# Turned features of the last stage: two more tiles turned on VectorE, and the blocks moved inside SBUF in place of a trip through DRAM

## The chip, the cores and the metric

The kernel runs on one NeuronCore of a Trainium2 chip. The core has TensorE (PE in the profile, its weight loads PEld), VectorE (DVE), ScalarE (ACT), GpSimd (POOL) and SyncE (SP), a scratch memory SBUF of 128 partitions, and PSUM, into which TensorE writes. Transfers are issued by an engine's queue (here mostly SP and POOL) and carried out by 16 DMA engines that all queues share. The metric is the device time of one execution in microseconds (us).

## What is computed

Two branches read the same layer-normed input, and both are added to it (sequence 2048, width 512, all in 32-bit floats):

```
xn  = layernorm(x)
q, k, v = heads(xn @ wqkv)                     # 32 heads of 16
phi(t)  = [softmax(t @ w_phi), softmax(-t @ w_phi)]   # 32 features a head
o   = phi(q) (phi(k)^T v) / (phi(q) (phi(k)^T 1) + 1e-6)
A   = o @ wo
z1, z2 = halves of gelu(xn @ w_in)             # 688 columns each
B   = (z1 * (w_sp @ layernorm(z2) + b_sp)) @ w_out
out = x + A + B
```

## The kernel before

The 2048 rows are 16 tiles of 128. Every large product is made of three matmuls: both operands are split into a rounded part (`round_h`, line 46, on ScalarE) and the rest (`rest_l`, line 51, on VectorE), and `mm3` (line 54) adds high x high, high x rest and rest x high. So in the profile L56, L57 and L58 are nearly all matmuls, L48 nearly all roundings and L52 nearly all rests.

The work has three stages. The first (about 0 to 190 us) norms and transposes x, makes q, k and v, the features of both (the exponentials and the reciprocals of their sums; the query side goes to DRAM, `e_d`, unscaled) and the sums over the keys. The second makes the w_sp product as a seven-product block scheme (`products`, `drain`, line 771 on), in 32 steps of which four make one pair of output tiles, and gates it (`gate`, line 797); the gated pair goes to DRAM already turned, features on partitions (`u_d`, `ur_d`).

The last stage, which the change is about, is the loop at line 1064, from about 485 us to the end. It takes the tiles in pairs i, i + 1. For each pair TensorE does, in this order: `project_u(i)` (gated values times w_out), `attend` (L997: 32 small matmuls of the features with the key sums), `project_u(i + 1)`, and `project_o` for both tiles (attention times wo, into the same PSUM tile). ScalarE copies the sum out (L1029), and POOL issues a store that adds it to the output, which holds x already (L1030). The next pair's attention needs its features *turned*: features on partitions, tokens along the row. How that is done depends on the tile:

- Tiles 0 and 1 are turned during the second stage: VectorE transposes every 32 x 32 block (`turn_q`, L561), four POOL stores (L563) put the blocks in their places in a DRAM buffer `q_d`, and SP loads them (L906).
- Tiles 2 to 7 (`s < TQ`, TQ = 8) stay as they are. Tiles 4 to 7 are copied by POOL into a tile of another type (L945, `er<-et`). `attend_T` (line 965) transposes them on TensorE, sixteen 128 x 128 transposes a pair (L980 for pair 2, L982 for pairs 4 and 6), and ScalarE copies the result out of PSUM in four pieces (L984).
- Tiles 8 to 15 take the way of tiles 0 and 1, but in this stage: the transpose L561, four stores of 128 KB (L563), and one load of 512 KB into the operand tile `f` (L939). The load waits for the four stores.

Before that, each tile's features are finished on VectorE (`q_fin`, line 541): a product with the key sums (L545), a reduction (L546), four small operations (L547 to L550), and the scaling of the 1024 features (L552). `ahead` (line 1054) runs behind each `project_o(i)`: it loads the features of tile i + 5 (L538), the gated values of tile i + 4 (L836, L837), and calls `features(i + 3)`. So the features of tile 11 are finished and turned while pair 8 and 9 is being projected.

The order in each engine's queue is not written out by hand: a planner runs a simulated time line over the instructions in the order of the program and puts on each queue what is ready, the earlier in the program first; `tc.issue_after(ins)` holds what follows behind one instruction of the same queue. Each queue then runs in that fixed order, and an instruction at its head that waits holds up everything behind it. The operand tiles `er` and `f` share three buffers (`er_pair`, line 925); the tile that VectorE transposes into (`qtmp`) is one of a ring of 16 (`slot`, line 825).

During this stage there is one more piece of VectorE work: the last pair's gate (line 1087, behind pair 6), whose z1 tile is loaded (line 1084) behind the transfer kept in `lasts[6]`.

Of the kernel before, what the change touches and what calls it, by code (L numbers as in the profile page):

```python
# [10 lines left out]
F32 = mybir.dt.float32  # L11
# [7 lines left out]
P = 128  # L19
S, D, H, DH, FH = 2048, 512, 32, 16, 688  # L20
NT = S // P
# [3 lines left out]
NF = 2 * D  # L25
# [3 lines left out]
BL = 32  # L29
# [11 lines left out]
def mixer(ctx: ExitStack, tc: tile.TileContext, x, x_t, wv, wqkT, phi_bd, wo, w_in, wst, b_r, w_out, out):  # L41
    nc = tc.nc
    pe, act, dve, pool, sp = nc.tensor, nc.scalar, nc.vector, nc.gpsimd, nc.sync
# [31 lines left out]
    dram = ctx.enter_context(tc.tile_pool(name="dram", bufs=1, space=DRAM))  # L75
# [3 lines left out]
    ur_d = dram.tile([NT, 2 * REM, P], F32, name="ur_d")  # L79
    kvT_d = dram.tile([P, D], F32, name="kvT_d")  # L80
    zb_d = dram.tile([P, NF], F32, name="zb_d")
    q_d = dram.tile([NT, P, NF], F32, name="q_d")
    nm_d = dram.tile([NT, ND, P], F32, name="nm_d")

    ident = cst.tile([P, P], F32, name="ident")
# [91 lines left out]
    with ExitStack() as p0:  # L177
# [236 lines left out]
        t = xz_tile(2 * D, F32R, "xT").rearrange("p (a b) -> p a b", a=2)  # L414
        xT.append(t)
        x0, pts = xt.pop(0), []
        for k in range(2):
            pts.append(ps.tile([P, 2, P], F32, tag="mm", name="pt"))
            for c in range(2):
                i = pe.transpose(pts[k][:, c], x0[:, (2 * k + c) * P:(2 * k + c + 1) * P], ident).ins  # L420
            keep(pe=i)
        warm_up(2)
        for cs, pt in zip(halves, pts):
            src = pt.rearrange("p a b -> p (a b)")
            i = round_h(act, t[:, 0, cs], src)
# [7 lines left out]
        p = ps.tile([P, D], F32, tag="mm", name="proj")  # L433
# [7 lines left out]
        p = ps.tile([P, D], F32, tag="mm", name="proj")  # L441
# [18 lines left out]
        p = ps.tile([P, D], F32, tag="mm", name="proj")  # L460
# [90 lines left out]
                          den.unsqueeze(2).to_broadcast([P, H, 2]), op=ALU.mult)  # L551
        return e, dve.tensor_tensor(heads(e), heads(e), bc(w, 2 * H), op=ALU.mult).ins  # L552

    TQ = 8

    NB = NF // P
    QB = NB * BL

    def turn_q(s, dst, e, eng):

        dve.transpose(dst.rearrange("p (m c t) -> p m c t", c=NB, t=BL), e.rearrange("p (c m j) -> p m c j", c=NB, j=BL))  # L561
        for b in range(P // BL):
            eng.dma_start(q_d[s, :, b * QB:(b + 1) * QB].rearrange("(m j) w -> j m w", j=BL),  # L563
                          dst[b * BL:(b + 1) * BL].rearrange("p (m w) -> p m w", w=QB))

    QC = 4
    NQ = NT // QC
# [45 lines left out]
    with ExitStack() as p1:  # L613
# [44 lines left out]
        for s in range(NE):  # L658
            et = load_q(s, tb.tile([P, QW], F32, name="et") if s else tmp1.tile([P, 4, D], F32, tag="zhl", name="et").rearrange("p a b -> p (a b)")[:, :QW])
            tmp = zw.tile([P, 4, FC], F32, tag="z2", bufs=2, name="qtmp").rearrange("p a b -> p (a b)")[:, :NF]  # L660
            e, _ = q_fin(et, tmp, zb)
# [57 lines left out]
    for s in range(NT):  # L719
        p = zproj((kv_ps_p, zc, zbp, za)[s % 4], s, w2, (0, 1) if s % 2 == 0 else (1, 0))  # L720
# [6 lines left out]
        z = z2[n][:, 2 * (s % 2):2 * (s % 2) + 2]  # L727
# [140 lines left out]
    for n in range(NC):  # L868
        i = SEQ[n][0]
        if n % NQ == 1 and i < NP - 1:  # L870
            z = load_z1(i)
        products(n, g)
        if n % NQ == NQ - 1 and i < NP - 1:
            c = gt.tile([P, 2, FU], F32, tag="c", name="c")
            cq = c[:, :, :FH].rearrange("p k (j f) -> p k j f", j=2)
            cb = drain(i, g, cq)
            g = {}
        if n + 3 < NC:
            raw[n + 3] = load_a(n + 3)
        if n + 2 < NC:  # L880
            A[n + 2] = prep_a(n + 2, raw.pop(n + 2))
        if n % NQ == NQ - 1 and i < NP - 1:
            turn = gate(i, cb, z, c, z, prep_a.last)
            if i < NP - 2:
                turn()
            if i in (2, 4):
                s = i // 2 - 1
                e, t = (gt.tile([P, 2, FU], F32, tag=tag, name=name).rearrange("p k f -> p (k f)")[:, :NF]
                        for tag, name in (("c", "c"), ("z1", "z1t")))
                pool.dma_start(e, e_d[s, :, :NF])  # L890
                turn_q(s, t, e, pool)
        if n == NC - 4:
            stage_w()
        if n == NC - 3:
            zs = slot("zb", F32R)
            zb, ident_r = zs[:, :NF].bitcast(F32), zs[:, NF:NF + P]
            round_h(act, ident_r, ident)
            sp.dma_start(zb, zb_d)
            uT = [first_gate(0)]
            ets[2] = load_q(2, slot("et"))  # L900
            es[2], last = q_fin(ets.pop(2), slot("qtmp")[:, :NF], zb)
        if n == NC - 2:
            fq = [slot("f")[:, :NF].rearrange("p (k b c t) -> p k b c t", k=2, c=NB // 2, t=BL) for h in range(2)]
            for k in range(2):
                for h in range(2):
                    sp.dma_start(fq[h][:, k], q_d[k].rearrange("p (b h w) -> h p b w", h=2, w=QB // 2)[h])  # L906
            t = xz_tile((KF + 1) * P, F32R, "u1")
            us = {1: load_u(1, t[:, :KF * P].bitcast(F32), t[:2 * REM, KF * P:(KF + 1) * P])}
    cb = drain(NP - 1, g, slot("c").rearrange("p (k j f) -> p k j f", k=2, j=2))
    with tc.issue_after(cb[2]):  # L910
        turn()
    mid.close()


# [13 lines left out]
    def features(s):  # L928
        with tc.issue_after(fin[-1]):
            tmp = slot("qtmp")[:, :NF]  # L930
            es[s], ins = q_fin(ets.pop(s), tmp, zb)
        fin.append(ins)
        if s == 3:
            return
        if s >= TQ:
            if s % 2 == 0:
                ft[s] = er_pair("f").bitcast(F32)
            turn_q(s, tmp, es.pop(s), pool)
            sp.dma_start(ft[s - s % 2][:, s % 2], q_d[s])  # L939
            return  # L940
        e = es[s]
        if s % 2 == 0:
            ep[s] = er_pair("er")
        es[s] = ep[s - s % 2][:, s % 2]
        lasts[6] = pool.dma_start(es[s].bitcast(F32), e).ins  # L945
# [117 lines left out]
    p, nxt = {}, dict(enumerate(uT))  # L1063
# [61 lines left out]
```

## Time and profile before

| | us |
|---|---|
| three runs, median (lowest to highest) | 620.32 (619.74 to 622.54) |
| the profiled execution | 618.58 |
| its span, first to last instruction | 616.8 |
| PE busy in the span | 607.8 |
| DVE busy in the span | 519.0 |
| ACT busy in the span | 261.5 |
| POOL busy in the span | 134.2 |

The mean granted clock of TensorE in that execution was 0.998. In rows of instructions the first numbers are the start and the length in us from the start of the span; "L561" is line 561 of the kernel, `qtmp<-et` is output and input by the program's names, and what stands in brackets is how long the engine was idle before and what ended it. A row of a group gives the count, the shortest, median and longest time in ns, and the first and last start. The rows of DMA issues give the count, the size of each, and the median us from issue to landing.

### The profile page before, as it was taken

The numbers are of one execution on the slowest core, as the hardware profiler recorded it, in microseconds if no ns is written. First come the engines' busy times: TensorE is split into PE (matmuls) and PEld (weight loads), VectorE is DVE, ScalarE is ACT, GpSimd is POOL, SyncE is SP. The second block draws the span as 40 slices with busy tenths as digits, with TensorE's granted clock in tenths as the row PEclk, the third lists the DMA queues.
The fourth block names the chain that finished last, engine by engine and source line by source line (L and its number), as shares of the span: only waits on it lengthen the run. The fifth ranks groups of instructions, "written<-read, shape, count | busy, mean of one in ns | idle before, by whom it ended". The sixth has DMA issues, their size and how long they took to land.

```text
span 616.8 us, 11392 instructions
## 1 busy us (share of the span) xinstructions
PE 607.8 (99%) x4286; PEld 554.4 (90%) x4286; DVE 519.0 (84%) x929; ACT 261.5 (42%) x416; POOL 134.2 (22%) x236
## 2 busy tenths in 40 slices
PE   8999999999999999999999999999999999999996
PEld 7888888888889999999999999999999987777775
DVE  5999999999978398989889896877879999999821
ACT  5653334323523467876434443342435343332221
POOL 4122232232110015442000002000100032344420
PEclk9999999999999999999999999999999999999999
DMA  8557876666446768001463745555566799999772
GB/s 315 192 136 165 227 178 170 159 163 169 125 143 162 255 224 289 2 1 35 149 142 124 191 96 177 135 157 145 165 182 215 214 345 306 322 272 264 188 172 58
DMA packets 58415, 109.95 MB, mean 178 GB/s; under 512 B 12457, under 2 KB 24617, under 8 KB 58121
## 3 DMA queue, kind: packets, MB, share of 16 engines
q1 hardware_dynamic: 43400, 64.96, 34.4%
q0 software_dynamic: 12656, 38.64, 25.1%
q10 hardware_dynamic: 2304, 5.64, 2.3%
q8 instruction: 33, 0.54, 0.3%
q14 instruction: 22, 0.17, 0.1%
HBM read 66.85 MB, written 35.80 MB: 166 GB/s over the span
## 4 chain that ended last, share of the span: by engine, by line
PE 95%; DMA 2%; issue 0%; DVE 0%; ACT 0%; SPq 0%; POOL 0%; DVEq 0%; ACTq 0%; POOLq 0%
PE g L58 11%; PE g L57 11%; PE g L56 11%; PE proj L57 7%; PE proj L56 7%; PE proj L58 7%; PE zps L56 6%; PE zps L57 6%; PE zps L58 6%; PE pout L56 6%; PE pout L58 5%; PE pout L57 5%; PE po L997 1%; DMA wst__2228<-in_w_in 1%; PE kvps L355 1%; PE pout L1011 1%
## 5 line engine op out<-in xcount | busy, mean ns | idle before, releaser
L57 PE MATMUL g<-B,A 128*128 128x344 f32 x448 | 143.3, 320 | 0.0
L56 PE MATMUL g<-B,A 128*128 128x344 f32 x448 | 142.9, 320 | 0.0
L58 PE MATMUL g<-B,A 128*128 128x344 f32 x448 | 140.4, 321 | 0.1
L56 PEld LDWEIGHTS g<-B,A 128*128 128x128 f32 x448 | 84.3, 188 | 0.1
L57 PEld LDWEIGHTS g<-B,A 128*128 128x128 f32 x448 | 84.2, 188 | 0.0
L58 PEld LDWEIGHTS g<-B,A 128*128 128x128 f32 x448 | 83.6, 188 | 0.4 <-DVE A L52 0.4
L48 ACT ACTIVATE A<-S 128x512 fp32r<-128x512 f32 x64 | 39.5, 630 | 78.7 <-DVE S L603 53.7
L56 PE MATMUL proj<-wqk_h,xT 128*128 128x512 f32 x128 | 50.1, 391 | 0.0
L58 PE MATMUL proj<-wqk_h,xT 128*128 128x512 f32 x128 | 49.8, 389 | 0.0
L57 PE MATMUL proj<-wqk_l,xT 128*128 128x512 f32 x128 | 49.8, 389 | 0.0
L123 ACT ACTIVATE e<-e,r_x 128x1024 f32<-128x1024 f32 x26 | 29.8, 1148 | 42.3 <-DVE e L122 41.2
L52 DVE TENSOR_TENSOR A<-S,A 128x512 fp32r<-128x512 f32 x64 | 43.0, 684 | 3.1 <-ACT A L48 2.8
L48 ACT ACTIVATE A<-wf 128x512 fp32r<-128x512 f32 (+1 forms) x64 | 32.9, 516 | 24.9 <-DMA wf<-in_wst 19.0
L56 PE MATMUL zps<-w_0h,xT 128*128 128x344 f32 x128 | 40.9, 320 | 0.1
L57 PE MATMUL zps<-w_1l,xT 128*128 128x344 f32 x128 | 40.8, 319 | 0.0
L57 PE MATMUL zps<-w_0l,xT 128*128 128x344 f32 x128 | 40.8, 319 | 0.0
L58 PE MATMUL zps<-w_0h,xT 128*128 128x344 f32 x128 | 40.8, 318 | 0.0
L56 PE MATMUL zps<-w_1h,xT 128*128 128x344 f32 x128 | 40.7, 318 | 0.0
L58 PE MATMUL zps<-w_1h,xT 128*128 128x344 f32 x128 | 40.6, 319 | 0.0
L52 DVE TENSOR_TENSOR A<-wf,A 128x512 fp32r<-128x512 f32 (+1 forms) x64 | 35.1, 551 | 3.7 <-ACT A L48 3.7
L126 DVE TENSOR_REDUCE sm<-e 128x64 f32<-128x1024 f32 x26 | 31.1, 1199 | 2.5 <-ACT e L123 2.5
L768 POOL DMA_DIRECT2D z1t<-z_d x16 | 8.7, 552 | 108.8 <-DMA wf<-in_wst 71.8
(224 smaller groups left out, 1435.4 us busy)
## 6 DMA issues: line engine op xcount, KB each, us to landing
wf<-in_wst SPq DMA_DIRECT2D x64, 256.0 KB, 3.2
e_d<-e POOLq DMA_DIRECT2D x16, 544.0 KB, 4.8
et<-e_d SPq DMA_DIRECT2D x16, 544.0 KB, 7.2
z_d<-z1f ACTq DMA_DIRECT2D x16, 344.0 KB, 3.1
z1t<-z_d POOLq DMA_DIRECT2D x16, 344.0 KB, 4.3
zacc<-e POOLq DMA_DIRECT2D x10, 512.0 KB, 4.9
u<-u_d SPq DMA_DIRECT2D x15, 320.0 KB, 4.9
xt<-in_x SPq DMA_DIRECT2D x16, 256.0 KB, 4.3
```

Of the source, the lines that this page charges most:

```text
L48: return act.activation(h, src, AF.Copy).ins
L52: return (eng or dve).tensor_tensor(l, src, h.bitcast(F32), op=ALU.subtract).ins
L56: pe.matmul(dst, ah, bh, start=start, stop=False)
L57: pe.matmul(dst, ah, bl, start=False, stop=False)
L58: return pe.matmul(dst, al, bh, start=False, stop=stop).ins
L123: softmax_pair.last = less, act.activation(e, e, AF.Exp, scale=scale).ins
L126: dve.tensor_reduce(sm, heads(e), axis=AX.X, op=ALU.add)
L355: i = pe.matmul(kv_acc[k:k + QP, m // 4], vs[:, m * QP:(m + 1) * QP], e[:, m * HP:(m + 1) * HP], start=first and m < 4 and len(ready) == n ...
L768: pool.dma_start(t[:, k, :FH], z1_d[2 * i + k])
L997: lasts[3] = pe.matmul(po[r][c * QP:(c + 1) * QP, k], kvT[rows, m // 2, cols], fs[m // 4][rows, m // 2 % 2], start=True, stop=True).ins
L1011: lasts[2] = pe.matmul(p, rt, w, start=False, stop=i == NT - 1 and k == 1).ins
```

## The change

Three things change, all in how features get turned.

1. TQ goes from 8 to 6: tiles 6 and 7 are now turned by VectorE too. Their copies L945, their sixteen TensorE transposes L982 and four ScalarE copies L984 are gone.
2. In the last stage (tiles 6 to 15) the transposed tile no longer goes to `q_d` and back. `move_q` sends each of the 4 x 4 pieces of 32 partitions x 256 elements (32 KB) straight from the transposed tile into the operand tile: sixteen transfers a tile, eight issued by SP (even b) and eight by POOL (odd b).
3. `q_d` keeps only tiles 0 and 1, whose way through DRAM stays as it was (`turn` and `store_q` together do what `turn_q` did). The name `turn` of the gate's second half becomes `turn_u`.

Since `lasts[6]` is set only where the copy L945 is issued, the load of z1 for the last gate now stands behind tile 5's copy and not tile 6's.

```diff
-    q_d = dram.tile([NT, P, NF], F32, name="q_d")
+    q_d = dram.tile([2, P, NF], F32, name="q_d")
...
-    TQ = 8
+    TQ = 6
...
-    def turn_q(s, dst, e, eng):
-
+    def turn(dst, e):
         dve.transpose(dst.rearrange("p (m c t) -> p m c t", c=NB, t=BL), e.rearrange("p (c m j) -> p m c j", c=NB, j=BL))
+
+    def store_q(s, t):
         for b in range(P // BL):
-            eng.dma_start(q_d[s, :, b * QB:(b + 1) * QB].rearrange("(m j) w -> j m w", j=BL),
-                          dst[b * BL:(b + 1) * BL].rearrange("p (m w) -> p m w", w=QB))
+            pool.dma_start(q_d[s, :, b * QB:(b + 1) * QB].rearrange("(m j) w -> j m w", j=BL),
+                           t[b * BL:(b + 1) * BL].rearrange("p (m w) -> p m w", w=QB))
+
+    def move_q(f, t):
+        for b in range(P // BL):
+            for m in range(P // BL):
+                move_q.last = (sp if b % 2 == 0 else pool).dma_start(f[m * BL:(m + 1) * BL, b * QB:(b + 1) * QB],
+                                                      t[b * BL:(b + 1) * BL, m * QB:(m + 1) * QB]).ins
...
                 pool.dma_start(e, e_d[s, :, :NF])
-                turn_q(s, t, e, pool)
+                turn(t, e)
+                store_q(s, t)
...
             if s % 2 == 0:
                 ft[s] = er_pair("f").bitcast(F32)
-            turn_q(s, tmp, es.pop(s), pool)
-            sp.dma_start(ft[s - s % 2][:, s % 2], q_d[s])
+            turn(tmp, es.pop(s))
+            move_q(ft[s - s % 2][:, s % 2], tmp)
             return
```

6 lines of the change are left out of this document (3 added, 3 removed).

## The prediction

> **What bounds the kernel now.** I read the page first (engine totals, the chain that ended last), then the last stage in stretches of 10 us, because every edited line runs there, then the chain of waits in order of time, and last the timelines of VectorE, POOL and SP around the one gap that the chain shows.
>
> ```profile
> span 616.8 us, 11392 instructions
> PE 607.8 (99%) x4286; PEld 554.4 (90%) x4286; DVE 519.0 (84%) x929; ACT 261.5 (42%) x416; POOL 134.2 (22%) x236
> ...
> PE 95%; DMA 2%; issue 0%; DVE 0%; ACT 0%; SPq 0%; POOL 0%; DVEq 0%; ACTq 0%; POOLq 0%
> ```
>
> TensorE is busy for 99% of the span and 95% of the closing chain is its own work. So a change pays only where it takes work off TensorE or closes one of its few gaps. The stretches say where a gap is; the columns are busy us of PE, PEld, DVE, ACT and POOL, then the granted clock, the busy share of the DMA engines, and GB/s.
>
> ```profile
> 540.00:550.00 10.00, 10.00 (x72) 7.60 (x71) 9.61 (x15) 3.81 (x5) 3.99 (x8) 1.00 0.97 268
> 550.00:560.00 10.00, 10.00 (x72) 7.64 (x71) 9.96 (x17) 3.03 (x5) 3.76 (x6) 1.00 1.02 270
> 560.00:570.00 10.00, 10.00 (x46) 8.17 (x44) 9.73 (x16) 2.25 (x4) 4.44 (x8) 1.00 0.94 270
> 570.00:580.00 10.00, 8.42 (x65) 6.38 (x64) 7.94 (x13) 2.25 (x4) 2.63 (x5) 1.00 0.81 222
> 580.00:590.00 10.00, 10.00 (x72) 7.67 (x71) 8.42 (x12) 3.02 (x5) 6.34 (x10) 1.00 0.77 157
> ```
>
> Here TensorE, VectorE and the DMA engines are all nearly full, and TensorE stands still once, for 1.58 us between 570 and 580. The chain of waits names the place, and the rows of L997 say for what:
>
> ```profile
> 536.09 1.34 PE ptq L982 x16
> ...
> 541.39 1.02 PE po L997 x32
> ...
> 570.34 1.58 issue
> 571.92 1.10 PE po L997 x32
> ...
> 586.47 1.02 PE po L997 x32
> ...
> 600.94 1.02 PE po L997 x32
> ```
>
> ```profile
> L997 PEldq EVENT_SEMAPHORE  x1: 5757/5757/5757, 566.1 to 566.1; - x1
> ```
>
> Every L997 group is the attention of one pair of tiles. The group at 571.92 is pair 10 and 11, and its queue stood in a semaphore wait from 566.1 to 571.86. What it waited for is the turned operand tile of tile 11, which goes VectorE transpose, four POOL stores to DRAM, SP load:
>
> ```profile
> 556.93 1.24 DVE L561 STREAM_TRANSPOSE qtmp<-et 128x1024 f32<-128x1024 f32 x1
> ```
>
> ```profile
> 558.47 2.25 POOL L563 DMA_DIRECT2D q_d<-qtmp  x4 [4.61 <-DVE qtmp L561]
> ```
>
> ```profile
> 565.53 0.34 SPq L939 DMA_DIRECT2D f<-q_d  x1
> ```
>
> The transpose ends at 558.17, the stores are issued from 558.47 to 560.72, the load can start only at 565.53, and the tile is there at 571.86: 13.7 us after the transpose, of which some 11 are two trips of a transfer.
>
> **The change part by part.** *Tiles 6 and 7 leave TensorE.* Sixteen transposes on TensorE (1.34 us at 536.09, on the path) go, and with them four ScalarE copies out of PSUM (L984), which nobody waits for because ScalarE is idle for more than half of these stretches. TensorE then reaches pair 6 at 541.39 - 1.34 = 540.05 and pair 10 at 570.34 - 1.34 = 569.0.
>
> *VectorE gets two more transposes.*
>
> ```profile
> 531.23 1.22 DVE L545 TENSOR_TENSOR qtmp<-et,zb 128x1024 f32<-128x1024 f32 x1
> ...
> 533.10 1.24 DVE L561 STREAM_TRANSPOSE qtmp<-et 128x1024 f32<-128x1024 f32 x1
> 534.26 1.18 DVE L546 TENSOR_REDUCE et<-qtmp 128x64 f32<-128x1024 f32 x1
> ...
> 573.73 1.29 DVE L52 TENSOR_TENSOR oT<-po,oT 128x512 fp32r<-128x512 f32 x2 [0.49 <-ACT oT L48]
> ...
> 577.23 0.83 DVE L52 TENSOR_TENSOR ul<-u,uh 128x640 fp32r<-128x640 f32 x1 [1.47 <-ACT uh L48]
> ...
> 585.27 1.25 DVE L561 STREAM_TRANSPOSE qtmp<-et 128x1024 f32<-128x1024 f32 x1
> ```
>
> One takes 1.16 us of the queue (533.10 to 534.26), two take 2.32. The stretches show VectorE with 9.6 to 10 us of work in every 10 up to 570, so nothing absorbs this before tile 11: its transpose ends at 558.17 + 2.32 = 560.49. Later 0.49 + 1.47 = 1.96 us of idle time (573.73, 577.23) take most of it back, so tile 15 is late by 0.36 only.
>
> *The trip through DRAM becomes one hop.* For tiles 6 to 15 sixteen transfers of 32 partitions x 1 KB replace the stores and the load; eight go through SP (even b), eight through POOL (odd b). No row shows such a transfer, so I bound its two costs. Issue: the four stores take 2.25 / 4 = 0.56 us each on POOL, and eight in a row on the same queue kept that pace, as did the 32-partition stores on SP; the rows are those, then the durations of all stores of q_d, then three of landing:
>
> ```profile
> 492.45 2.35 POOL L818 DMA_DIRECT2D u_d<-z1t  x4 [34.92 <-DVE z1t L814]
> 494.78 2.25 POOL L820 DMA_DIRECT2D ur_d<-z1t  x4
> ```
>
> ```profile
> L818 SPq DMA_DIRECT2D u_d<-zt x4: 330/518/782, 553.1 to 558.4; - x4
> ```
>
> ```profile
> L563 POOL DMA_DIRECT2D q_d<-qtmp x32: 550/572/937, 534.6 to 588.5; - x32
> ```
>
> ```profile
> wof<-in_wo SPq DMA_DIRECT2D x16, 64.0 KB, 2.9
> ```
>
> ```profile
> er<-et POOLq DMA_DIRECT2D x4, 512.0 KB, 7.7
> ```
>
> ```profile
> DMA to landing us min/median/max: 5.6/7.7/9.6
> ```
>
> So the eighth starts 7 x 0.56 = 3.9 us after the first, on POOL as on SP; the bounds are 0.33 (the shortest on SP) and 0.94 (the longest store on POOL). Landing: small loads of 64 KB took 2.9, and the one SBUF to SBUF copy of this stage, 512 KB, 7.7, with 5.6 and 9.6 as its ends (the last row is of that copy, L945). I take 5.3: that is what tile 11's own stores needed from the start of the fourth (558.47 + 3 x 0.56 = 560.15) to the load's start, less the short dispatch, under the same load on the DMA engines. It is the nearest row in shape, place and time; 2.9 and 9.6 stay as ends. Then tile 11 is there at 560.49 + 0.30 (transpose to first issue, as 558.17 to 558.47) + 3.9 + 5.3 = 570.0. TensorE arrives at 569.0 and waits 1.0 in place of 1.58; it starts pair 10 at 570.0 and not at 571.92: **1.9 us gained** in all.
>
> ```profile
> 523.75 1.23 DVE L552 TENSOR_TENSOR et<-et 128x1024 f32<-128x1024 f32 x1
> ...
> 530.09 1.22 DVE L552 TENSOR_TENSOR et<-et 128x1024 f32<-128x1024 f32 x1
> ```
>
> ```profile
> 570.16 1.24 DVE L561 STREAM_TRANSPOSE qtmp<-et 128x1024 f32<-128x1024 f32 x1
> ```
>
> ```profile
> 586.81 2.22 POOL L563 DMA_DIRECT2D q_d<-qtmp  x4 [0.74 <-DVE qtmp L561]
> ```
>
> ```profile
> 595.01 0.32 SPq L939 DMA_DIRECT2D f<-q_d  x1
> ```
>
> The other pairs by the same terms. Tile 13 (transpose 570.16 + 1.24 = 571.40): 571.40 + 2.32 + 0.30 + 3.9 + 5.3 = 583.2, needed at 586.47 - 1.9 = 584.6. Tile 15: 585.27 + 1.25 + 0.36 + 0.30 + 3.9 + 6.5 (what its own stores took, from 588.47 to the load at 595.01) = 597.6, needed at 600.94 - 1.9 = 599.0. Tile 7: its scaled features are done at 523.75 + 1.23 = 524.98; tile 6's transpose adds 1.16, and between scaling and the end of the transpose lay 3.0 us in tile 8 (531.31 to 534.34); 529.2 + 0.30 + 3.9 + 5.3 = 538.7, needed at 540.05. All three have 1.3 to 1.4 us left, so they are next to wait if landing is slower than I take it.
>
> ```profile
> L1030 POOL DMA_DIRECT2D out<-xr x15 | 14.1, 967 | 45.7 <-ACT xr L1029 44.7 <-ACT f L984 1.0
> ```
>
> *What the queues lose.* POOL gets 8 issues a tile for 4 (or for 1, the copy of tiles 6 and 7). Queued behind them are the accumulating stores of the output (L1030, two a pair, 0.97 us each); a pair takes 586.47 - 571.92 = 14.5 us, and 16 x 0.56 + 2 x 0.97 = 10.9, so POOL keeps room. SP gets 8 a tile for 1; its head waits for the transpose where it waited for the stores to land, which is earlier, and behind it stand the loads of features and gated values, fetched two to four tiles ahead. At 0.52 each (the median of L818 on SP) and six loads a pair at the 0.34 of the row at 565.53, SP is at 16 x 0.52 + 6 x 0.34 = 10.4 of 14.5.
>
> ```profile
> L997 PEldq EVENT_SEMAPHORE  x1: 51/51/51, 598.7 to 598.7; - x1
> ```
>
> *Edits at nothing.* q_d is smaller, names change. The load of z1 for the last gate (L1084) is held behind the last er copy, now tile 5's and not tile 6's; it may start some us earlier, and nothing needs it before that gate, two pairs of tiles on. A matmul that reads the operand tile must now wait for up to 16 semaphores where it waited for one; one that is met costs 0.05 us, 0.8 for 16, which is hidden because that wait stood at 598.7, 2.2 us ahead of its matmuls; without that cover it is 0.8 a pair.
>
> **The sum.** The profiled execution took 618.58, its span 616.8, so 1.8 lies around the span. Span 616.8 - 1.9 = 614.9, execution 616.7. The median of the runs shown is 620.32, 1.7 above the profiled one; carried over, the forecast is 620.32 - 1.9 = **618.4**. What a measurement here can tell from no change is about 0.5%, 3.1 us, so this is a gain below that.
>
> **The rivals.** *The whole stall goes.* If landing takes 4.3 or less from the last issue (the 2.9 row is in that region, and the traffic falls, since each tile's 512 KB is moved once and not twice), tile 11 is in time, and 1.34 + 1.58 = 2.9 is gained: 617.4. Against it: DMA engines 94 to 102% busy up to 570, and tile 11's own stores needed 5.3.
>
> ```profile
> 546.13 0.69 DVE L52 TENSOR_TENSOR oT<-po,oT 128x512 fp32r<-128x512 f32 x1
> ```
>
> ```profile
> 547.97 0.40 PE L58 MATMUL pout<-woh,oT 128*128 128x512 f32 x1
> ```
>
> *VectorE becomes the bound.* It is 2.32 later and TensorE 1.34 earlier, so the rest of the attention output (L52 into oT) of pair 6 shifts 3.7 us against TensorE. It ended at 546.82 and its first matmul that needs the second half ran at about 548 (row at 547.97), 1.2 us later; if the planner keeps the order, TensorE waits 3.7 - 1.2 = 2.5 us there, and reaches pair 10 at 571.5: 0.4 gained, 619.9. Against it: the order is planned anew, and this work stands ahead of the features in it.
>
> *SBUF to SBUF transfers land like the er copies.* At 7.7 tile 11 comes at 572.4, 0.5 later than now: 620.8. At 9.6 it comes at 574.3: 2.4 later, 622.7; the other pairs wait less than that, and waits on one path do not add up. For it: in this stage no other row has both ends in SBUF. Against it: that copy is 16 times as large and was issued in the fullest stretch.
>
> *The issuing queues become the bound* (the other side). Sixteen transfers and two output stores a pair are 10.9 us of POOL at 0.56. From 0.78 us each on (14.5 less the two output stores, over 16) POOL no longer keeps up and every pair from 6 on is late. At 0.94, the longest store, a pair takes 16 x 0.94 + 1.94 = 17.0 us, 2.5 too many; over the four intervals from pair 6 to pair 14 that is 10, less the 2.9 that could be gained: 620.3 + 7.1 = 627. For it: such stores exist, in the stretch where the new transfers go. Against it: their median is 0.57, and the groups of four and eight quoted ran at 0.56 to 0.59.
>
> [...]
>
> **How the numbers follow.** Forecast as worked out (618.4): 0.45. Whole stall gone (617.4): 0.22. VectorE (619.9): 0.10. Slow landing (620.8 to 622.7): 0.14. Queues (627, or more): 0.09. Faster by over 0.5% means below 617.2: about half of the second case and a little of the first, 0.14. Slower means above 623.4: the queues, a third of the slow landings and what a new plan can upset, 0.17. The rest, 0.69, is within 0.5%. The range leaves out the queues and the outer part of the second case: from 616.8, 0.6 below the full gain, as the lowest run shown is below the median, to 622.8, the slow end of landing.
>
> **What would show it.** Right: sixteen L982 matmuls fewer, ten L561 transposes in the last stage, the gap before pair 10's L997 near 1 us, tile 11's last transfer starting 4 to 5 us after its transpose and landing about 5 later. Wrong: no gap or over 2 us there; a gap before pair 6, 8, 12 or 14; transfers over 0.78 us apart on POOL or SP; matmuls of L58 waiting for oT; output stores piling up behind waiting transfers.

## The result and the profile after

The changed kernel is slower: 628.09 us (median of 6, 623.69 to 631.23) against 621.09 for the kernel before in the same runs, ratio 1.0114, interval 1.0076 to 1.0151. That is about 7 us lost where 1.9 gained was forecast, beyond the slow end of 622.8. The profiled execution took 625.95, its span 623.9 against 616.8: 7.1 us longer. The ratios further down leave out single executions of 1548, 2130 and 3431 us; that of 2130 is the profiled one of e11, so there is no usable trace of e11.

First the page of the changed kernel: the head with the engine totals, then the closing chain.

```profile
span 623.9 us, 11541 instructions
PE 612.1 (98%) x4270; PEld 556.0 (89%) x4270; DVE 521.3 (84%) x931; ACT 260.9 (42%) x412; POOL 154.7 (25%) x282
...
PE 88%; DMA 5%; DVE 4%; ACT 1%; issue 1%; SPq 0%; POOL 0%; ACTq 0%; POOLq 0%
```

TensorE has 16 instructions fewer and is busy 4.3 us longer: part of its work has become slower. Its share of the closing chain fell from 95% to 88%; DMA and VectorE now release it. The stretches of the last stage (same columns as in the prediction):

```profile
520.00:530.00 10.00, 7.97 (x60) 6.29 (x66) 8.04 (x11) 3.40 (x6) 5.41 (x10) 0.83 0.87 261
...
540.00:550.00 10.00, 10.00 (x70) 7.60 (x69) 9.02 (x14) 3.55 (x6) 8.20 (x16) 1.00 1.00 261
550.00:560.00 10.00, 9.88 (x55) 7.38 (x54) 9.96 (x16) 2.85 (x5) 4.45 (x9) 1.00 0.70 167
560.00:570.00 10.00, 9.40 (x52) 7.09 (x53) 9.76 (x17) 1.98 (x4) 5.68 (x12) 1.00 0.73 182
570.00:580.00 10.00, 9.28 (x64) 6.27 (x63) 9.83 (x13) 3.03 (x5) 7.65 (x15) 1.00 1.01 247
```

From 550 to 570 the traffic did fall (167 and 182 GB/s where it was 270), POOL is busier in every stretch (8.20 us of the ten from 540 on where it was 3.99), and between 520 and 530 TensorE is idle for 2 us and its granted clock is 0.83. The chain of waits shows every attention group (L1005 is the old L997) and what came between its halves:

```profile
515.37 7.43 DMA er<-et
...
529.53 1.02 PE po L1005 x32
...
544.00 1.45 PE po L1005 x29
...
558.88 1.04 PE po L1005 x16
559.95 0.60 ACT oT L48
560.60 0.50 PE pout L56
561.09 0.23 PE pout L57
561.33 1.00 PE po L1005 x16
...
575.32 1.04 PE po L1005 x16
...
577.76 1.00 PE po L1005 x16
...
591.75 1.48 PE po L1005 x32
...
606.70 1.45 PE po L1005 x29
```

Set beside the same view of before, each start is later by:

| pair | before | after | later by | added since the pair ahead |
|---|---|---|---|---|
| 4 | 525.48 | 529.53 | 4.05 | 4.05: 0.6 that was there at pair 2, 2.03 of a wait, 1.4 of a slow clock behind it |
| 6 | 541.39 | 544.00 | 2.61 | -1.44: the sixteen transposes are gone |
| 8 | 555.87 | 558.88 | 3.01 | 0.40: pair 6's group took 1.45 and not 1.02 |
| 10 | 571.92 | 575.32 | 3.40 | 0.39: pair 8's split group costs 1.97 (0.39 + 1.58), the old wait of 1.58 is gone |
| 12 | 586.47 | 591.75 | 5.28 | 1.88: pair 10's split group |
| 14 | 600.94 | 606.70 | 5.76 | 0.48: pair 12's group |
| end | 616.8 | 623.9 | 7.1 | 1.3: pair 14's group 0.43, the rest behind it |

Two things are new. First the wait before pair 4, in TensorE's timeline (the changed kernel):

```profile
520.37 0.46 PE L990 MATMUL ptq<-zb,er 128*128 128x128 f32 x4
522.85 1.57 PE L990 MATMUL ptq<-zb,er 128*128 128x128 f32 x12 [2.03 <-DMA er<-et]
...
525.63 0.63 PE L56 MATMUL pout<-wu,uh 128*128 128x512 f32 x1
526.06 0.63 PE L57 MATMUL pout<-wu,uh 128*128 128x512 f32 x1
```

Tile 5's copy took 7.43 us from 515.37 (it was needed at 520.8). Behind the wait matmuls of one size start 0.43 us apart (525.63, 526.06) and not 0.23 as in the chain of waits at 561.09: TensorE's granted clock is 0.50 from 523.3 to 526.7. The forecast had priced a wait at its own length.

Second the split groups. In the changed kernel's queue the 16 attention matmuls of rows 0 to 63 stand ahead of the 16 of rows 64 to 127 in pairs 6 to 14, and in pairs 8 and 10 two L56/L57 matmuls stand between them that need the first half's output, rounded by ScalarE (`559.95 0.60 ACT oT L48` in the chain). TensorE idles 0.72 us there, and the halves no longer run beside each other: 1.04 + 1.00 for 1.02 (one of these matmuls takes 0.38 us in the median, and a whole group of 32 took 1.02). The planner made this order anew. Together the cut groups are some 5.2 us of this execution (0.4 for pairs 6, 12 and 14 each, 2.0 for 8 and 10), the wait with its slow clock is 3.4.

Against the signs that the prediction named: sixteen transposes on TensorE are gone and ten stand on VectorE, but there is no wait before pair 10, because TensorE is 3.4 us late there itself. Tile 11's transpose ended at 565.03, where 560.49 was forecast, and SP issued its share of the transfers from 568.65 on (timelines of VectorE and SP):

```profile
563.79 1.24 DVE L560 STREAM_TRANSPOSE qtmp<-et 128x1024 f32<-128x1024 f32 x1
...
568.65 4.97 SPq L570 DMA_DIRECT2D f<-qtmp  x8
```

The last one starts 8.0 us after the transpose, where 4 to 5 was named, and the tile is there at 575.0, 10.0 after the transpose; 9.5 had been forecast for this trip.

### The profile page after: what moved, and what is told of

Same layout as the page of the kernel before. It is cut to its first block, busy times and chain, and to the rows that moved or that the text cites. A ratio compares the mean times of both kernels' runs of the same rounds, so it can differ in the third digit from the quotient of the medians.

```text
span 623.9 us, 11541 instructions
## 1 busy us (share of the span) xinstructions
PE 612.1 (98%) x4270; PEld 556.0 (89%) x4270; DVE 521.3 (84%) x931; ACT 260.9 (42%) x412; POOL 154.7 (25%) x282
## 4 chain that ended last, share of the span: by engine, by line
PE 88%; DMA 5%; DVE 4%; ACT 1%; issue 1%; SPq 0%; POOL 0%; ACTq 0%; POOLq 0%
PE g L58 10%; PE g L57 10%; PE g L56 10%; PE proj L56 7%; PE proj L57 7%; PE proj L58 7%; PE zps L56 6%; PE zps L57 6%; PE zps L58 6%; PE pout L56 4%; PE pout L57 4%; PE pout L58 4%; PE po L1005 2%; DMA wf<-in_wst 1%; DMA wst__2228<-in_w_in 1%; PE kvps L355 1%
## 5 line engine op out<-in xcount | busy, mean ns | idle before, releaser
L57 PE MATMUL g<-B,A 128*128 128x344 f32 x448 | 143.3, 320 | 0.0
L56 PE MATMUL g<-B,A 128*128 128x344 f32 x448 | 143.0, 320 | 0.1
L56 PEld LDWEIGHTS g<-B,A 128*128 128x128 f32 x448 | 84.3, 188 | 0.4 <-ACT A L48 0.4
L57 PEld LDWEIGHTS g<-B,A 128*128 128x128 f32 x448 | 84.2, 188 | 0.0
L48 ACT ACTIVATE A<-S 128x512 fp32r<-128x512 f32 x64 | 39.6, 629 | 72.6 <-DVE S L610 53.5
L56 PE MATMUL proj<-wqk_h,xT 128*128 128x512 f32 x128 | 50.1, 391 | 0.0
L57 PE MATMUL proj<-wqk_l,xT 128*128 128x512 f32 x128 | 49.8, 389 | 0.0
L52 DVE TENSOR_TENSOR A<-S,A 128x512 fp32r<-128x512 f32 x64 | 43.1, 684 | 3.8 <-ACT A L48 3.6
L48 ACT ACTIVATE A<-wf 128x512 fp32r<-128x512 f32 (+1 forms) x64 | 33.0, 517 | 30.3 <-PE g L58 15.1
L570 POOL DMA_DIRECT2D f<-qtmp x80 | 40.7, 581 | 17.5 <-DMA f<-qtmp 6.1
L56 PE MATMUL zps<-w_0h,xT 128*128 128x344 f32 x128 | 41.0, 320 | 0.3 <-ACT z1f L153 0.3
L57 PE MATMUL zps<-w_1l,xT 128*128 128x344 f32 x128 | 40.8, 319 | 0.0
L57 PE MATMUL zps<-w_0l,xT 128*128 128x344 f32 x128 | 40.8, 318 | 0.0
L56 PE MATMUL zps<-w_1h,xT 128*128 128x344 f32 x128 | 40.7, 318 | 0.0
L52 DVE TENSOR_TENSOR A<-wf,A 128x512 fp32r<-128x512 f32 (+1 forms) x64 | 35.1, 551 | 3.1 <-ACT A L48 3.1
```

The costliest lines, as they stand in the source:

```text
L48: return act.activation(h, src, AF.Copy).ins
L52: return (eng or dve).tensor_tensor(l, src, h.bitcast(F32), op=ALU.subtract).ins
L56: pe.matmul(dst, ah, bh, start=start, stop=False)
L57: pe.matmul(dst, ah, bl, start=False, stop=False)
L570: move_q.last = (sp if b % 2 == 0 else pool).dma_start(f[m * BL:(m + 1) * BL, b * QB:(b + 1) * QB], t[b * BL:(b + 1) * BL, m * QB:(m + 1) ...
```

## The experiments

All ratios are to the kernel before, run beside it on the same chip (its medians there were 619.3 to 621.1). "Tied" means that each attention matmul is held behind the one before it, so that a group can't be cut.

| label | base and edit | median us | ratio (95%) |
|---|---|---|---|
| e1_z1_early | before, z1 load behind tile 5's copy | 619.82 | 1.000 (0.9961 to 1.0038) |
| e2_rows_apart | before, rows 0 to 63 first | 620.56 | 1.0006 (0.997 to 1.0043) |
| e3_z1_late | after, z1 load behind tile 6's transfers | 631.67 | 1.018 (1.014 to 1.022) |
| e4_rows_together | after, tied | 625.64 | 1.0081 (1.0056 to 1.0107) |
| e5_both | after, z1 late, tied | 625.98 | 1.0096 (1.0064 to 1.0127) |
| e6_moves_only | before with the transfers, TQ 8 | 626.63 | 1.0101 (1.0046 to 1.0155) |
| e7_moves_together | e6, tied | 621.28 | 1.0016 (0.9985 to 1.0047) |
| e8_tq6_dram | before, TQ 6, through DRAM | 628.93 | 1.0142 (1.0095 to 1.019) |
| e9_vector_alone | before, two unread VectorE transposes | 627.08 | 1.0092 (1.006 to 1.0125) |
| e10_vector_relieved | e4, two reductions less | 625.30 | 1.0068 (1.0033 to 1.0103) |
| e11_sp_free | e7 with nine `rt` buffers | 626.87 | 1.0091 (1.0058 to 1.0125) |
| e12_all_relieved | e10 with nine `rt` buffers | 628.40 | 1.0122 (1.009 to 1.0155) |
| e13_vector_swapped | e9, two reductions less | 619.49 | 0.9995 (0.9957 to 1.0032) |
| e14_fewer_turned | before, TQ 10 | 619.66 | 0.9997 (0.9978 to 1.0016) |
| e15_changed_again | after | 627.61 | 1.013 (1.0088 to 1.0173) |

### First theory: two side effects

The first theory took the two new things in the trace for the cause: the z1 load that moved ahead, beside tile 5's copy, and the order of the attention matmuls. Each was put into the kernel before by itself.

```diff
-        lasts[6] = pool.dma_start(es[s].bitcast(F32), e).ins
+        ins = pool.dma_start(es[s].bitcast(F32), e).ins
+        if s < 6:
+            lasts[6] = ins
```

> The kernel before, with one thing of the change alone: the two loads of z1 for the last gate are issued behind tile 5's er copy and not behind tile 6's. Theory S (side effects of the change, not the transfers, cost the time; this is its first part): the loads, 688 KB, share the DMA engines with tile 5's copy, which lands about 2 us late; TensorE stands still some 2 us before pair 4's L982, then runs at a spacing of about 0.43 us a matmul for a few us, 3.6 us in all; 1.6 of it is given back because the wait before pair 10 (1.58) is then covered. So 2 us slower than before, about 623. Rival Q (the sixteen small transfers and their queues cost the time): no difference from before, no gap at pair 4.

Between pairs 2 and 4 no wait of half a us came up, and the time stayed. That part of the theory falls.

```diff
-        for m in range(H // 2):
+        for m in [*range(0, H // 2, 2), *range(1, H // 2, 2)]:
```

> The kernel before, with the 16 attention matmuls of each pair in another order: the eight on rows 0 to 63 first, then the eight on rows 64 to 127, where before they alternate. Theory S, second part: two matmuls on different halves of the rows run beside each other, so a group apart takes 2.04 us in place of 1.02; eight groups, 8.2 us, less the 1.58 of the wait before pair 10 that the five groups ahead of it cover: 6.6 us slower, 627.7. Rival: the order inside a group is of no weight: 621, groups of 1.02.

The group took 1.12 in place of 1.09 us by TensorE's timeline, not 2.04, and the time stayed: the order by itself cost 0.03 us of the group here, where nothing stands between the halves.

The reverse, in the changed kernel: the z1 load back behind the first turned tile, the groups tied, and both.

```diff
         move_q(ft[s - s % 2][:, s % 2], tmp)
+        if s == TQ:
+            lasts[6] = move_q.last
```

> The changed kernel, with the load of z1 put behind tile 6's last POOL transfer (as before it stood behind tile 6's copy). Theory S: the gap of 2.03 us before pair 4's second half and the slow matmuls behind it go, 3.6 us: 624.5 against 628 for the changed kernel, 0.5% slower than before. Rival Q: the gap is from the new transfers in the queues, and stays: 628.

It did not help (1.018 against 1.0114 for the changed kernel, the intervals overlap). TensorE waited for a turned tile before pair 8 (its timeline in e3):

```profile
562.28 1.93 PE L1007 MATMUL po<-f,kvT 64*32 64x256 f32 x16 [5.41 <-DMA f<-qtmp]
```

Half a group took 1.93, at a granted clock of 0.50 that lasted to about 573.

```diff
+            with tc.issue_after(lasts[3] if m else lasts[2]):
-            lasts[3] = pe.matmul(po[r][c * QP:(c + 1) * QP, k], kvT[rows, m // 2, cols], fs[m // 4][rows, m // 2 % 2],
-                                 start=True, stop=True).ins
+                lasts[3] = pe.matmul(po[r][c * QP:(c + 1) * QP, k], kvT[rows, m // 2, cols], fs[m // 4][rows, m // 2 % 2],
+                                     start=True, stop=True).ins
```

> The changed kernel, with the 16 attention matmuls of a pair tied to one another in the order of the program, so that the planner can't put the first half of the rows ahead of the second. Theory S: the groups of pairs 6 to 14 go back to 1.02 us from 1.45 to 2.05, and the two waits of 0.72 for ScalarE in pairs 8 and 10 go: 3.4 + 1.4 = 4.8 us, 623.3 against 628. Rival Q: the planner split the groups because the second half of the rows does land late; tied together the group waits as long as it gains, and the time stays within 1 us of 628.

All groups were whole again (1.09), and 0.8% was still lost. TensorE now waited for VectorE's half of the attention output (timeline of e4):

```profile
563.42 0.52 PE L58 MATMUL pout<-woh,oT 128*128 128x512 f32 x1 [1.72 <-DVE oT L52]
...
582.18 0.50 PE L58 MATMUL pout<-woh,oT 128*128 128x512 f32 x1 [2.40 <-DVE oT L52]
```

That is the wait of the rival "VectorE becomes the bound". e5 put both edits (of e3 and e4) in:

> The changed kernel with both repairs: z1 loaded behind tile 6's transfers, and the attention matmuls tied together. Theory S: everything lost comes back, 3.6 + 4.8 = 8.4 us off the changed kernel, and what is left is the forecast's second case, TensorE transposes and the wait before pair 10 gone: about 618.5 to 619.5, 0.3% below the kernel before. Rival Q: the transfers cost by themselves; it stays above the kernel before, at 623 or more.

It stayed at 625.98. TensorE waited 0.98, 3.33 and 1.04 for turned tiles in the groups of pairs 6, 8 and 12. Mending what the trace named first brought up another wait each time, which suggests that something behind them is late as a whole.

### Second theory: VectorE's queue

The change was then taken apart. e6 has the transfers with TQ at 8 (no more work for VectorE), e7 the same tied.

```diff
-            turn_q(s, tmp, es.pop(s), pool)
-            sp.dma_start(ft[s - s % 2][:, s % 2], q_d[s])
+            turn(tmp, es.pop(s))
+            move_q(ft[s - s % 2][:, s % 2], tmp)
```

> The changed kernel with TQ back at 8: tiles 6 and 7 as before, only the sixteen transfers in place of the trip through DRAM (z1 stands behind tile 6's copy again). Theory S: no gap at pair 4; the planner splits the groups of pairs 10 and 12, about 1.7 us each, and orders two others badly, 0.4 each, 4.3 us; the wait before pair 10, 1.58, goes: 2.7 us slower than before, 623.8. Rival Q: four fifths of the transfers are there, so four fifths of the loss: 626.5.

> As the run with TQ at 8 and the sixteen transfers, with the attention matmuls tied together. Theory S: the groups take 1.02 again, the wait before pair 10 is gone: 1.6 us faster than before, 619.5. Rival Q: as without the tie, 626.

e7 is as fast as before (ratio 1.0016). So the hop inside SBUF by itself cost nothing here; nor did it gain. SP's timeline in e7 says why, for tile 11, whose transpose ended at 560.1:

```profile
563.62 0.43 SPq L538 DMA_DIRECT2D et<-e_d  x1
564.98 0.32 SPq L843 DMA_DIRECT2D u<-u_d  x1
565.40 5.41 SPq L570 DMA_DIRECT2D f<-qtmp  x8
```

SP's eight transfers start 5.3 us after the transpose, behind the stores of the gated pair and loads that were waiting, and take 5.4 us to issue where eight on POOL take 4.0. TensorE waited 1.03, and its group took 1.75 in place of 1.10, since the last piece landed at 573.6, when the group had begun. That is 13.5 us after the transpose; through DRAM it was 13.7.

e6 lost 1% with the same transfers in an order that the planner was free to choose (its runs spread from 622 to 630, and the two intervals just touch): SP's eight start at 566.35 there, and before pair 10 TensorE waits

```profile
575.37 1.93 PE L1005 MATMUL po<-f,kvT 64*32 64x256 f32 x16 [4.65 <-DMA rt<-ur_d]
```

and its granted clock is 0.50 to about 585. e8 is the other half of the change, TQ at 6 with the trip through DRAM kept (and z1 behind tile 6's stores); e9 is less still, the two transposes alone, whose result nobody reads while TensorE keeps its own.

```diff
-    TQ = 8
+    TQ = 6
```

> The kernel before with TQ at 6 and the trip through DRAM kept (z1 behind tile 6's first stores). Theory S: TensorE saves 1.34, VectorE is 2.32 later, the trip is as long as it was (13.7 us for tile 11), so tile 11 lands at 574.2 and pair 10 starts 2.3 us later than before; a wait of about 3 us also falls before pair 6, and where a wait passes 2 us the matmuls behind it run slower, some 1.5 us: 623.4 to 625. Rival D (VectorE's two transposes cost nothing): 1.34 faster, 619.7.

```diff
         e = es[s]
+        if s > 5:
+            dve.transpose(tmp.rearrange("p (m c t) -> p m c t", c=NB, t=BL), e.rearrange("p (c m j) -> p m c j", c=NB, j=BL))
```

> The kernel before (TQ 8, trip through DRAM), with two more VectorE transposes, of tiles 6 and 7, whose result nobody reads: VectorE's share of the change and nothing else. Theory V (VectorE is full from 502 to 573, and what it gets more comes back as waits of TensorE): 2.3 us later at tile 11, the wait before pair 10 grows from 1.6 to about 3.9, and may halve the clock behind it for some us: 2.3 to 5 us slower than before, 622 to 625. Rival T (the transfers of tiles 6 and 7 and the queues that carry them): no transfer is added, 619.5 as before.

Both lose about as much as the whole change, and more than was expected of them. The 2 us from which e8's expectation lets the matmuls run slower were an estimate from the changed kernel's 2.03; in e4 the clock was 0.50 behind 1.72 and 1.00 behind 2.40. TensorE's timeline of e8, at pair 10:

```profile
578.34 1.96 PE L999 MATMUL po<-f,kvT 64*32 64x256 f32 x32 [6.52 <-DMA f<-q_d]
```

and of e9, with matmuls behind the wait that start 0.42 apart:

```profile
577.93 1.96 PE L999 MATMUL po<-f,kvT 64*32 64x256 f32 x32 [5.47 <-issue]
...
582.12 0.63 PE L58 MATMUL pout<-wu,ul 128*128 128x512 f32 x1
582.54 0.63 PE L56 MATMUL pout<-wu,uh 128*128 128x512 f32 x1
```

Nothing but VectorE's work has changed in e9, and the wait of 1.58 has become 5.47. (TensorE and ScalarE keep their order; the planner put some transfers of SP and POOL elsewhere, but tile 11's trip is no longer for that: 13.5 us from its transpose to TensorE's start, 13.7 before.) VectorE's timeline of e9 shows how 2.3 us of work become more:

```profile
551.76 1.58 DVE L803 TENSOR_TENSOR z1t<-z1t,c 128x1376 f32<-128x1376 f32 x1
553.26 1.23 DVE L561 STREAM_TRANSPOSE qtmp<-et 128x1024 f32<-128x1024 f32 x1
...
558.10 0.82 DVE L52 TENSOR_TENSOR ul<-u,uh 128x640 fp32r<-128x640 f32 x1 [0.52 <-ACT uh L48]
...
562.01 1.28 DVE L52 TENSOR_TENSOR oT<-po,oT 128x512 fp32r<-128x512 f32 x2
563.21 1.23 DVE L561 STREAM_TRANSPOSE qtmp<-et 128x1024 f32<-128x1024 f32 x1
```

and of the kernel before, behind tile 11's transpose:

```profile
559.19 1.28 DVE L52 TENSOR_TENSOR oT<-po,oT 128x512 fp32r<-128x512 f32 x2
```

Tile 11's transpose ends at 564.44 where it ended at 558.17: 6.27 later. TensorE was itself 2.13 late by pair 4 in this execution, all of it from ahead of the first added transpose (523.09), so 4.14 of the 6.27 count. At the end of tile 9's transpose (544.09, before 540.12) it is 1.8 by the same reckoning, about what the two transposes take. The other 2.3 come between tile 9 and tile 11: the attention output of pair 8 (L52 into oT, some 1.2) now stands ahead of tile 11's transpose and stood behind it, and the queue stops longer for ScalarE (0.62 at 548.75 and 0.52 at 558.10, before 0.29 once). The first product of the last gate (L803) also moved, ahead of tile 10's transpose (before, that transpose came at 546.73 and the gate at 549.72); it stands ahead of tile 11's in both.

The wait grew by 3.89. The slow clock added 2.59 (from pair 10 to pair 12 it is 17.14 us in e9 and 14.55 before). 2.13 + 3.89 + 2.59 are the 8.6 by which the span is longer; without the 2.13 it is 6.5, and the medians differ by 6.0.

Then VectorE was relieved in the changed kernel: e4 without the two reductions (L546) of tiles 6 and 7.

```diff
-        dve.tensor_reduce(t, heads(tmp), axis=AX.X, op=ALU.add)
-        dve.tensor_tensor(t, t, r, op=ALU.mult)
+        if not less:
+            dve.tensor_reduce(t, heads(tmp), axis=AX.X, op=ALU.add)
+        dve.tensor_tensor(t, r if less else t, r, op=ALU.mult)
```

> The changed kernel with the attention matmuls tied together, and the reduction L546 left out for tiles 6 and 7, so that their normalizers are not computed: 2 x 1.2 us less of VectorE's work, as much as the two transposes add. Theory V: the waits of TensorE for oT, 1.72 and 2.40 us, go, and the slow matmuls behind one of them: 619 to 621, against 625.6 with all the work. Rival T: the transfers are all there, so it stays at 625 to 626.

It took 625.30, so the expectation missed. The waits for VectorE's half went, and right behind them stood another (timeline of e10):

```profile
573.54 2.40 PE L1007 MATMUL po<-f,kvT 64*32 64x256 f32 x32 [3.46 <-DMA f<-qtmp]
```

Tile 11's transpose ended at 557.52 here and at 560.10 in e7, and SP began its transfers at 565.85 and 565.40, at the same place in either. So beside VectorE the queue of SP is a second limit in the changed kernel, and less work on VectorE alone does not bring the time back. e11 and e12 tried to free SP's head from the `rt` loads (e7, and e10, each with nine buffers in place of six):

```diff
-                      cw.tile([2 * REM, P], F32R, tag="rt", bufs=6, name="rt"))
+                      cw.tile([2 * REM, P], F32R, tag="rt", bufs=9, name="rt"))
...
-    wk.tile([P, 10 * QP], F32, tag="gap", name="gap")
+    wk.tile([P, 3 * QP], F32, tag="gap", name="gap")
```

> TQ at 8, the sixteen transfers, the attention matmuls tied together, and nine buffers in place of six for the small loads rt, which stand on SP ahead of the transfers and wait there until TensorE has read the buffer (a dummy tile is smaller, to make room). Theory H (SP's head is held by such a load while tile 11's blocks are ready): the transfers of tile 11 start on SP within 1 to 2 us of its transpose and not 5.3 later, the wait of 1.0 us before pair 10 goes: 1 us less than with six, 620.3. Rival: another transfer holds SP instead, the wait stays, 621.3.

> The changed kernel with everything so far: attention matmuls tied together, the reduction L546 left out for tiles 6 and 7 (their normalizers are not computed), nine buffers for rt. Theories V and H: no wait of TensorE over 0.5 us from 510 on, and with the 16 transposes off TensorE the forecast's second case, 617 to 618.5, 0.2 to 0.4% below before. Rival T: 623 or more.

Both expectations missed. Why e11 is slow is open, for want of a trace. In e12 a new wait of 5.27 us at 504.30, for ScalarE's half of the attention output, ahead of everything that the edit was for, took the gain; and SP's head was not free, it began tile 11's transfers 7.6 us after the transpose. Whether a free SP would make the hop worth something is left open.

### Load or order

e9 left one doubt: was it VectorE's load, or did any edit of its queue bring a bad order? e13 is e9 with e10's two reductions left out: the two unread transposes stay, the load is that of before. e14 goes the other way, and e15 is the changed kernel once more.

> The kernel of e9 (before, with two unread transposes on VectorE for tiles 6 and 7), but the reduction of L546 (1.18 us of VectorE) is left out for tiles 6 and 7, so that part of their denominators is not computed. VectorE's work in the stage is then that of before to within 0.1 us, while the two extra transposes and every queue but VectorE's stay as in e9. Theory (it is VectorE's load ahead of tile 11 that costs): the transpose of tile 11 ends within 1.5 us of before's, the gap before pair 10 is 1 to 3 us, and the time is 619 to 622.5, ratio 0.997 to 1.003. Rival (it is what the edit does to the planned order, whatever the load): the gap before pair 10 stays at 4 to 5.5 us and the time at 625 to 628.

It is as fast as before, ratio 0.9995. Tile 11's transpose ended at 556.8, and before pair 10 TensorE waited 1.08, with no slow clock behind it (1.00 from 570 to 580):

```profile
570.94 1.10 PE L1000 MATMUL po<-f,kvT 64*32 64x256 f32 x32 [1.08 <-issue]
```

So it is not any edit of the queue that costs: 2.3 us more of VectorE's work ahead of tile 11, and 6 us are lost; take 2.4 away again, and they are back. But the order came back with the load: tile 10's transpose stands at 546.11 in e13, ahead of the gate at 549.10, and pair 8's attention output at 558.57, behind tile 11's transpose at 555.58. No run has the load of e9 in the order of before, so what the load costs by itself and what through the order planned for it is not told apart.

```diff
-    TQ = 8
+    TQ = 10
```

> Before with the bound TQ at 10 in place of 8: tiles 8 and 9 are turned on TensorE too, by way of DRAM only tiles 10 to 15. The opposite step of the change: TensorE has 16 transposes more (1.34 us), VectorE two transposes less (2.32 us). If the prices are those of the prediction (a wait costs its own length): +1.34, and the gap of 1.58 before pair 10 closes, because tile 11 is 2.3 us earlier and TensorE 1.3 later: 620.9, ratio 1.000. Theory as it stands (VectorE's load ahead of tile 11 counts for more than its own duration): tile 11's transpose ends 3 to 6 us earlier than before's, no gap before pair 10, and the time is again 619.5 to 621.5. Rival (this plan is chance: any edit of VectorE's queue in this stage costs some 6 us): 625 or more, with a gap of over 2 us at some pair.

TensorE has 16 transposes more and no wait at all; the interval from pair 8 to pair 10 in the chain of waits of e14 is 14.47, where it was 16.05:

```profile
557.16 1.02 PE po L997 x32
...
571.63 1.02 PE po L997 x32
```

1.34 paid, 1.58 saved: the same time within a fifth of a per cent. Tile 11's transpose ended at 556.20, 2.0 earlier and not the 3 to 6 of "theory as it stands": taking work out moved it by no more than that work's 2.3. The kernel before already lay between the two limits, and no version here beats it by what can be measured.

> The changed kernel once more, unedited. If its loss is made by the plan of its queues, the gap of about 2 us before pair 4 (waiting for the er copy of tile 5) and the cut attention groups of pairs 8 and 10 are there again, and the ratio is within 1.006 to 1.016. If the gap is made by the transfers' luck of one execution, it is missing or stands before another pair, and the split groups alone stay.

The ratio is 1.013 again, and pairs 8 and 10 are cut again; but no wait stands before pair 4. It stands before pair 8 (stretch and TensorE's timeline of e15):

```profile
560.00:570.00 10.00, 10.00 (x42) 6.61 (x42) 4.64 (x8) 1.34 (x2) 3.93 (x8) 0.67 0.65 167
```

```profile
557.90 1.07 PE L1005 MATMUL po<-f,kvT 64*32 64x256 f32 x16 [2.70 <-DMA f<-qtmp]
559.67 0.74 PE L56 MATMUL pout<-woh,oT 128*128 128x512 f32 x1 [0.71 <-ACT oT L48]
...
560.77 1.93 PE L1005 MATMUL po<-f,kvT 64*32 64x256 f32 x16
```

Where the wait falls is a matter of the execution, the loss is not. This fits what e1 found: z1 is loaded as early in e15 as in the first execution, without a wait before pair 4. That wait was one slow landing of tile 5's copy (7.43 us).

## Why the prediction was wrong

**The step that failed** is "VectorE gets two more transposes": one takes 1.16 us of the queue, two take 2.32, "so nothing absorbs this before tile 11: its transpose ends at 558.17 + 2.32 = 560.49". The price of the instruction was right and the fullness of the queue was seen; the error was to let a full in-order queue shift by just what is added. In e9 the same two transposes made tile 11 later by 4.14 relative to TensorE (6.27 by the clock of the span), because the order planned for the fuller queue puts other work ahead of it and the queue stopped longer for ScalarE. By the prediction's terms the wait before pair 10 would be 1.58 + 2.32 = 3.9 in e9 and 1.34 more in e8; it was 5.47 and 6.52. In the changed kernel the transpose ended at 565.03 and not 560.49. There TensorE was 3.0 late itself by pair 8, for the reasons of the next paragraphs, so that no wait for the tile shows.

**A wait was priced at its own length.** Behind a wait of 5.47 the clock added 2.6, behind 2.03 the changed kernel lost 1.4. No term of the sum held this, and the trace of before couldn't show it: its only wait (1.58) left the clock at 1.00. With it the gain of 1.34 for the sixteen transposes, which did come (-1.44 at pair 6), is outweighed by a wait 2 us longer.

**"The trip through DRAM becomes one hop" landed sooner than taken but began late.** These are the new transfers in the changed kernel (count, size, median us to landing; then ns that one issue takes, shortest, median and longest):

```profile
f<-qtmp SPq DMA_DIRECT2D x80, 32.0 KB, 4.1
f<-qtmp POOLq DMA_DIRECT2D x80, 32.0 KB, 4.4
```

```profile
L570 SPq DMA_DIRECT2D f<-qtmp x80: 507/589/1864, 523.3 to 598.1; - x80
L570 POOL DMA_DIRECT2D f<-qtmp x80: 496/498/1167, 524.1 to 596.0; - x80
```

5.3 had been taken for landing; 4.1 and 4.4 are the medians. The 5.3 was partly a queue: tile 11's four stores in the kernel before had landed 4.4 after their issue, by 564.6, and the load stood behind another one on SP until 565.53:

```profile
DMA to landing us min/median/max: 4.2/4.4/4.4
```

```profile
564.94 0.43 SPq L836 DMA_DIRECT2D u<-u_d  x1
```

An issue took 0.50 on POOL in the median, 0.56 had been taken; on SP it took 0.59, and eight with the pauses between them five to six and a half us, above the 3.9. What was missed is the start: SP began tile 11's transfers 3.6 us after the transpose in the changed kernel and 5.3 after it in e7, and not 0.30. The sentence that SP's head "waits for the transpose where it waited for the stores to land, which is earlier" leaves out the loads and gate stores ahead of it. So the trip of tile 11 was 10.0 in the changed kernel, near the 9.5 of the sum by luck (it starts 3.6 after the transpose and not 0.3, and the last one lands 2.0 after its issue and not 5.3). In e7 it was 13.5, so that 0.2 us of the 4.2 were gained (13.7 less 9.5).

**The planned order was taken as given.** "Edits at nothing" counted the semaphores of an operand that now comes in pieces, 0.05 us each; but only the kernels with the pieces have cut groups, and those of the changed kernel's trace are some 5.2 us. Each edit changed the order, up to SP's place for a tile's transfers (e6 against e7: the same work, 0.85% apart).

**The rivals.** "VectorE becomes the bound" had the right cause at a chance of 0.10 and a wrong price: 619.9, by way of a wait of 2.5 for oT. Such waits are there in e4 (1.72 and 2.40), but the time is 625.6: behind the first the granted clock was 0.50 (564 to 566), so that it took 3.6 (18.08 from pair 8 to pair 10, 14.47 without a wait), and the second was not in the sum. "The issuing queues become the bound" forecast 627, and that this is near the result is luck: it took 0.94 for an issue on POOL, which had 0.50 in the median and began each tile at most 1.5 us behind its transpose. The queue that came late was SP, up to 4.0 behind in the changed kernel. Where nothing held it up POOL issued eight of the small transfers in 3.9 us (from 531.91 on), with 4.4 from issue to landing in the median, so one did not wait out the other, and e7 with sixteen of them for each of tiles 8 to 15 costs nothing that can be measured. "Edits at nothing" held for z1 (e1).

What isn't settled: with the planner free the parts do not add up (transposes alone 0.9%, transfers alone 1.0%, both 1.1 to 1.3%). With whole groups they do within their intervals (transposes alone 0.9%, transfers 0.2%, both 0.8% in e4), so that the transposes are enough for most of the loss. But e10 and e12, which take VectorE's added work out of the changed kernel again, don't bring the time back. The runs fit one stretch of too little slack, with VectorE and SP near their limits, in which whatever is late first is made dearer by the clock; that reading is argued from them, not tested apart.

## What to carry to other kernels

Where an engine shows 9.6 to 10 us of work in every 10 and its last output is already waited for, an instruction added to it can cost more than its duration, as in e9 (4.1 us for 2.3, while 2.3 less gave 2.0 in e14): look what stands behind it in the queue and what the consumer's wait costs once it is longer. Take a step apart before trusting the trace's first name for the loss: here the wait named (tile 5's copy) moved from one execution to the next, and two unread transposes lost about as much as the whole change. The shorter trip gained only 0.2 us for tile 11 in e7 (13.5 for 13.7), because the queue that starts it was held up by something else for 5.3.

## What the runs showed of the hardware

*Half the clock followed some of TensorE's waits and not others.* The granted clock stayed at 1.00 behind waits of 0.98 and 1.04 (e5), 1.03 (e7), 1.08 (e13), 1.31 (e1), 1.58 (before), 1.73 (e8) and 2.40 (e4). It was 0.50 behind 1.65 (e12), 1.72 (e4), 2.03 (the changed kernel), 2.70 (e15), 3.46 (e10), 4.65 (e6), 5.27 (e12) and 5.41 (e3). Behind 5.47 (e9) equal matmuls started 0.42 apart, and behind 6.52 (e8) the attention group took 1.96; in the changed kernel they started 0.43 apart in place of 0.23. The clock stood at 0.50 for 3.4 us in the changed kernel (523.3 to 526.7), for 6.8 in e15 (559.8 to 566.6), for at least 9 in e6 (575 to 584) and 11 in e3 (562 to 573). The length of a wait alone does not separate the two here: 1.65 and 1.72 were enough, 1.73 and 2.40 were not. What decided is not shown.

*Transfers waited for others whose data they don't touch.* Among the waits of the changed kernel's queues from 520 to 600 (total us, times, longest) stand

```profile
POOL f L570 <- DMA f<-qtmp: 6.1, 5, 2.6
...
POOL f L570 <- DMA out<-xr: 1.9, 3, 1.2
```

where the second row is transfers that read nothing that the output stores write. The longest of them, 1.2 us, stood before tile 10's last piece on POOL (its start is 563.43). What ties the one to the other is not shown.
